# Spacing a single-channel gather a quarter of a step apart, and moving one batch's load and folds earlier, in an FFT and MLP kernel

## Chip, cores, metric

Each kernel runs on one core of a Trainium2 chip. The metric is device time in microseconds (us). Each timed run is one execution; a kernel's figure is the median of its runs. All timed runs quoted here were classed as fast. The experiments were timed in four groups, on three different chips, so every ratio is taken against runs of the kernel before in the same group. Two experiments (after_look and folds_look) are single runs for a trace, and a single run has no known state; they are marked where they are used, and no verdict rests on them alone.

## The reference, cut to what matters

```python
# x: (8, 3008, 256); w_in: (256, 2048); w_out: (2048, 256); all float32
X = np.fft.fft(np.fft.fft(x, axis=1), axis=2).real      # FNet mixing
h = X.reshape(24064, 256) @ w_in
g = np.where(h > 0, h, np.exp(np.minimum(h, 0)) - 1)    # ELU
out = g @ w_out
```

## The kernel before

The program is a pipeline of 376 steps (47 tiles of 512 tokens, eight steps each) of about 4.75 us; in the source a step is T = 4.8. The Fourier transform of the next batch and all side work are put between by a list of events, `at(time, function)`. `time` is only a place in program order. An instruction wrapped in `pin` keeps its place on its queue; an unpinned transfer may be moved along its queue by the scheduler. So the program order in the source is not the order of SyncE's queue.

The real transform uses symmetry, so channel 128 needs its own column of x: one element out of each row of 256, 8 batches by 3008 rows. Those elements are copied singly, 192 rows at a time ("a piece"), 4 pieces to a quarter. A finished quarter goes to a DRAM scratch tensor (`xe_dr`) and returns in another layout (`xs`):

```python
def load_ext(j, s0, s1):                       # quarter j, rows s0 to s1
    if j == 0 and s0 == 0:
        state["x1"] = spool.tile([128, HALF + 1], FP, tag="rx", bufs=1, name="x1")
    t = state["x1"][j * NB : (j + 1) * NB]     # 8 partitions, one per batch
    def copy(s0, s1, row, step):
        pin(nc.sync.dma_start(
            out=t[:, s0:s1],
            in_=bass.AP(tensor=xt, offset=x.offset + row * ND + 128,
                        ap=[[SEQ * ND, NB], [step * ND, s1 - s0], [1, 1]])))
    ...                                        # one quarter has a piece of a single row more
    if s1 == 768:
        nc.sync.dma_start(out=xe_dr[j], in_=t[:, 0:768])        # not pinned

def get_ext():
    xs = state["xs"] = spool.tile([128, 4, NB, 6], FP, tag="xs", bufs=1, name="xs")
    for j in range(4):                                          # not pinned
        nc.sync.dma_start(out=xs[:, j], in_=xe_dr[j].rearrange("b (p m) -> p b m", m=6))

def fold_ext():                                # GpSimd: three additions make xe
    ...
def dft_ext():                                 # TensorE: 24 matmuls with xe as weights
    ...
```

Four other parts share the queues. Two are DMA traffic: the stores of finished output tiles, 40 transfers for the first two tiles (24 of them 32 KB each, all on SyncE), and a later batch's x, in four transfers:

```python
def load_x(b):
    for j in (2, 1):                           # indirect loads, issued by GpSimd
        load = nc.gpsimd.indirect_dma_start(out=L[j], ...)
        if b == 1:
            pin(load)
    nc.sync.dma_start(out=L[3], in_=xrows(b, HALF, 6, 128))     # SyncE, 768 KB each
    nc.sync.dma_start(out=L[0], in_=xrows(b, 0, 6, 128))
```

Two are GpSimd work: folds (additions of x with its mirror image) and sums of weights. The events concerned:

```python
for i in range(8):
    at((13 + 0.6 * i) * T + 3.6, lambda i=i: sum_weights(i))
...
for n in range(16):
    j, k = divmod(n, 4)
    at((14.4 + 0.62 * n) * T, lambda j=j, k=k: load_ext(j, 192 * k, 192 * (k + 1)))
at(25.0 * T, get_ext)
at(26 * T + 1.35, fold_ext)
at(26 * T + 4.75, dft_ext)
...
for b in range(1, NB):
    s0 = (b - 1) * steps_b
    l0 = s0 - 8 if b > 1 else 5.2
    at(l0 * T + 0.1, lambda b=b: state.update(L=load_x(b)))
    f0, f1 = (s0 - 1, s0 + 38) if b > 1 else (8, 37)
    ...                                        # folds spread evenly over steps f0 to f1
```

## Time and profile before

| | before |
|---|---|
| median of 3 runs (range) | 1985.48 us (1985.08 to 1985.95) |
| TensorE busy, in the profiled run | 1958.8 of 1985.3 us |
| TensorE's wait for xe | 11.89 us, until 192.88 us |

The profiled run itself took 1987.05 us, 1.6 us more than the median; this will matter. The prediction below shows the lines of the slices, waits, stretches and SyncE's queue on which this table rests, and works out from them what the stall costs and how long the quarters of the gather took. One line is wanted beside them. It is from GpSimd's timeline of the kernel before (start, us, engine, line, operation, out<-in, count, and in brackets what ended the idle time ahead of it):

```profile
173.68 1.00 POOL L157 DMA_INDIRECT xl<-in_x_dram,ix  x1 [0.27 <-POOL o L476]
```

This is the first of GpSimd's own two loads of batch 2's x. It is issued 3.9 us after the last quarter's first piece, and on another queue than the gather's, so it cannot be seen in SyncE's queue. How the two kinds of view are read together decides this case: a queue's timeline tells when transfers are issued, and only the next entry that waits for them tells when they landed (the last four pieces left the queue by 181.46 us, 169.82 + 11.64; the xe_dr that waits for them was issued at 187.58).

### The profile page before, as it was taken

What the parts mean: (1) busy time and instruction counts of PE and PEld (TensorE: products, weight loads), DVE (VectorE), ACT (ScalarE), POOL (GpSimd) and SP (SyncE); (2) the same over time, 40 slices, a digit from 0 to 9 for tenths busy, and PEclk for the clock granted to TensorE, in tenths of its full rate; (3) what the DMA queues carried; (4) which work ended last, traced back from release to release, by engine and by line L of the source; (5) the groups of instructions that cost most, each with busy time, mean ns of one, the idle gap of its engine ahead of it and who ended that gap; (6) DMA issues with size and microseconds to landing.
All of it is one profiled execution on the core that took longest, in us unless ns stands there. A gap on an engine that the chain in (4) does not pass through costs nothing.

```text
span 1985.3 us, 26858 instructions
## 1 busy us (share of the span) xinstructions
PE 1958.8 (99%) x8912; PEld 1656.7 (83%) x8912; DVE 1278.8 (64%) x2325; ACT 869.4 (44%) x1668; POOL 1362.2 (69%) x1800
## 2 busy tenths in 40 slices
PE   9997999999999999999999999999999999999998
PEld 5786888888888888888888888888888888888887
DVE  8864666675666656666566665666566665566666
ACT  4643434444444444444444444444444444344443
POOL 3696757786587765877667875678757776455665
PEclk9998999999999999999999999999999999999999
DMA  8135111121001110011100211013010010100101
GB/s 331 54 34 60 44 16 17 39 59 21 13 15 51 43 30 13 18 43 46 28 11 19 59 30 27 11 19 85 10 21 11 19 22 14 16 12 12 22 10 24
DMA packets 255546, 71.01 MB, mean 36 GB/s; under 512 B 243934, under 2 KB 244850, under 8 KB 255024
## 3 DMA queue, kind: packets, MB, share of 16 engines
q1 hardware_dynamic: 250896, 56.46, 14.3%
q0 software_dynamic: 2336, 12.59, 2.0%
q8 instruction: 70, 1.15, 0.2%
q14 instruction: 68, 0.56, 0.1%
q10 hardware_dynamic: 2176, 0.26, 0.1%
HBM read 44.43 MB, written 24.80 MB: 35 GB/s over the span
## 4 chain that ended last, share of the span: by engine, by line
PE 94%; DVE 2%; DMA 2%; SPq 1%; POOL 1%; issue 1%; ACT 0%; POOLq 0%; DVEq 0%; ACTq 0%
PE H L382 38%; PE pD L382 16%; PE pB L382 16%; PE pC L382 16%; PE pA L382 8%; DMA x<-in_x_dram 1%; PE M L382 1%; SPq L988 1%; POOL G L391 1%; DVE E L764 0%; SPq L613 0%; DVE G L790 0%; DVE v L388 0%; DVE pow L281 0%; DVE Ir L388 0%
## 5 line engine op out<-in xcount | busy, mean ns | idle before, releaser
L391 POOL TENSOR_TENSOR G<-G 128x256 f32<-128x256 f32 x1440 | 1037.1, 730 | 545.0 <-DVE G L790 436.3
L764 DVE SCALAR_TENSOR_TENSOR E<-Rb,wex,H 128x256 f32<-128x256 f32 x752 | 327.8, 477 | 618.2 <-PE H L382 614.4
L394 ACT ACTIVATE G<-H 128x512 f32<-128x512 f32 x376 | 224.6, 597 | 951.1 <-DVE G L774 951.1
L382 PE MATMUL H<-Ir,Ws 128*128 128x256 f32 x1504 | 387.3, 380 | 1.3 <-DVE E L764 1.3
L382 PE MATMUL H<-Rr,Wc 128*128 128x256 f32 x1504 | 387.6, 380 | 0.0
L382 PE MATMUL pC<-G,WT 128*128 128x256 f32 x1440 | 369.5, 379 | 0.0
L382 PEld LDWEIGHTS H<-Rr,Wc 128*128 128x128 f32 x1504 | 285.0, 190 | 56.9 <-issue 4.0
L382 PEld LDWEIGHTS H<-Ir,Ws 128*128 128x128 f32 x1504 | 277.8, 189 | 50.3 <-DVE E L764 4.7
L382 PEld LDWEIGHTS pC<-G,WT 128*128 128x128 f32 x1440 | 273.6, 190 | 37.2
L774 DVE SCALAR_TENSOR_TENSOR G<-E,H 128x512 f32<-128x512 f32 x376 | 256.9, 683 | 39.5 <-PE H L382 2.9
L790 DVE SCALAR_TENSOR_TENSOR G<-G,H 128x512 f32<-128x512 f32 x376 | 255.5, 680 | 28.7 <-ACT G L394 28.6
L790 DVE SCALAR_TENSOR_TENSOR G<-M,G 128x512 f32<-128x512 f32 x376 | 256.6, 683 | 0.0
L394 ACT ACTIVATE G<-G 128x512 f32<-128x512 f32 x376 | 233.2, 620 | 0.0
L382 PE MATMUL pA<-G,w 128*128 128x256 f32 x784 | 229.4, 379 | 0.7 <-DVE G L790 0.7
L382 PE MATMUL pB<-G,w 128*128 128x256 f32 x784 | 229.3, 379 | 0.0
L382 PE MATMUL pD<-G,w 128*128 128x256 f32 x784 | 229.3, 379 | 0.0
L394 ACT ACTIVATE M<-G 128x512 f32<-128x512 f32 x376 | 223.9, 595 | 0.0
L394 ACT ACTIVATE M<-M 128x512 f32<-128x512 f32 x376 | 220.9, 588 | 0.0
L382 PE MATMUL pB<-G,WT 128*128 128x256 f32 x720 | 214.8, 380 | 3.2 <-POOL G L391 3.2
L382 PE MATMUL pD<-G,WT 128*128 128x256 f32 x720 | 214.4, 379 | 1.5 <-DVE v L388 1.5
L382 PEld LDWEIGHTS pA<-G,w 128*128 128x128 f32 x784 | 148.9, 190 | 21.3 <-DVE G L790 1.1
L382 PEld LDWEIGHTS pB<-G,w 128*128 128x128 f32 x784 | 149.0, 190 | 20.3
(140 smaller groups left out, 1407.9 us busy)
## 6 DMA issues: line engine op xcount, KB each, us to landing
out_dram<-ot SPq DMA_DIRECT2D x496, 32.0 KB
xl<-in_x_dram SPq DMA_DIRECT2D x16, 768.0 KB
out_dram<-ot SPq DMA_DIRECT2D x256, 2.0 KB
Rb<-r SPq DMA_DIRECT2D x10, 376.0 KB
raw<-in_moe_w_in_dram SPq DMA_DIRECT2D x7, 512.0 KB
MC<-dft_mats SPq DMA_DIRECT2D x3, 1131.0 KB
raw<-in_moe_w_out_dram SPq DMA_DIRECT2D x4, 512.0 KB
out_dram<-ot SPq DMA_DIRECT2D x64, 28.0 KB
```

What stands on the lines that cost most here:

```text
L382: nc.tensor.matmul(out_, lhsT=lhsT, rhs=rhs, start=start, stop=stop, skip_group_check=True)
L391: pin(nc.gpsimd.tensor_tensor(out=o, in0=a, in1=b, op=op))
L394: pin(nc.scalar.activation(out=o, in_=i, func=func, **kw))
L764: nc.vector.scalar_tensor_tensor(out=S.E[:, c], in0=Rb[:, cols(i)], scalar=wex[:, f : f + 1], in1=S.H[:, c], op0=ALU.mult, op1=ALU.add,)
L774: nc.vector.scalar_tensor_tensor(out=two(S.G[:, 0:512])[:, :, ::-1], in0=two(S.E), scalar=2.0, in1=two(S.H), op0=ALU.mult, op1=ALU.subtract,)
L790: nc.vector.scalar_tensor_tensor(out=o, in0=e, scalar=-1.0, in1=h, op0=ALU.add, op1=ALU.max)
L988: queue.dma_start(out=bass.AP(tensor=out.tensor, offset=out.offset + r0 * ND + half * 128 + 32 * g, ap=[[2 * ND, w], [64 * ND, nb], [1, 32 ...
```

## The change

The intent: close the gather up, so that it ends before TensorE wants it, and move GpSimd's work on batch 1 out of the time when TensorE waits for GpSimd. No arithmetic and no byte is added or removed.

```diff
     for i in range(8):
-        at((13 + 0.6 * i) * T + 3.6, lambda i=i: sum_weights(i))
+        at((12.9 + 0.5 * i) * T + 3.6, lambda i=i: sum_weights(i))
 ...
         at(
-            (14.4 + 0.62 * n) * T,
+            (14.4 + 0.25 * n) * T,
             lambda j=j, k=k: load_ext(j, 192 * k, 192 * (k + 1)),
         )
 ...
-        l0 = s0 - 8 if b > 1 else 5.2
+        l0 = s0 - 8 if b > 1 else 3.2
         at(l0 * T + 0.1, lambda b=b: state.update(L=load_x(b)))
-        f0, f1 = (s0 - 1, s0 + 38) if b > 1 else (8, 37)
-        at(f0 * T, lambda b=b: begin_folds(b))
+        first = (6, 7, 7, 8, 9, 9, 10, 10, 12, 15)
+
+        def fold_slot(n):
+            if b > 1:
+                return s0 - 1 + 39 * n // n_big
+            return first[n] if n < len(first) else 17 + int(0.92 * (n - len(first)))
+
+        at(fold_slot(0) * T, lambda b=b: begin_folds(b))
 ...
-            slot = int(f0 + n * (f1 - f0) / n_big)
+            slot = fold_slot(n)
```

## The prediction

> **What bounds the kernel now.** I read the page first. TensorE is busy 1958.8 of 1985.3 us, and the chain that ended last is 94% TensorE. So the floor of this program is about 1959 us, and a change that adds and removes no TensorE work can at best win back part of the 26.5 us in which TensorE is idle. The slices say where to look:
>
> ```profile
> PE   9997999999999999999999999999999999999998
> ...
> PEclk9998999999999999999999999999999999999999
> ```
>
> Each slice is 49.6 us. The fourth (149 to 198 us) is the only one below 9 in the TensorE row, apart from the last, and the only one whose granted clock is below 9. Next, the waits of 130 to 200 us, as engine, line, what it waited for, us in total, times, longest:
>
> ```profile
> POOL xs L391 <- DMA xs<-xe_dr: 13.2, 1, 13.2
> PEld H L382 <- POOL xe L391: 12.3, 1, 12.3
> PE H L382 <- POOL xe L391: 11.9, 1, 11.9
> ...
> PE pB L382 <- POOL G L391: 2.2, 2, 1.6
> ```
>
> TensorE stands still once for 11.9 us, because GpSimd has not made xe, because GpSimd waits 13.2 us for xs. That is the gather of channel 128: load_ext copies single elements of x into one tile, each quarter goes through DRAM (xe_dr) and returns as xs, fold_ext adds, dft_ext multiplies. The busy table by stretches (first columns: window, us, TensorE busy with its count; further on the granted clock) prices the stall:
>
> ```profile
> 181.00:184.60 3.60, 0.00 (x0) 0.00 (x0) 0.00 (x0) 0.85 (x2) 0.00 (x0) 1.00 0.80 3
> 184.60:192.80 8.20, 0.00 (x0) 0.00 (x0) 0.00 (x0) 0.00 (x0) 0.65 (x3) 0.50 0.43 105
> 192.80:198.30 5.50, 5.42 (x27) 2.50 (x28) 0.00 (x0) 1.17 (x3) 5.20 (x9) 0.50 0.00 0
> 198.30:205.00 6.70, 6.70 (x32) 5.86 (x32) 4.95 (x10) 1.98 (x4) 4.78 (x6) 1.00 0.41 122
> ```
>
> After 3.6 us of idleness the clock is halved, and the first 5.4 us of work run at half speed: another 2.7 us lost. The stall costs 11.9 + 2.7 = **14.6 us** in all. Last, the queue of SyncE that issues the gather (start, us in the queue, what, count):
>
> ```profile
> 113.58 6.30 SPq L613 DMA_DIRECT2D x<-in_x_dram  x4
> 126.05 0.28 SPq L631 DMA_DIRECT2D xe_dr<-x  x1
> 126.37 0.64 SPq L613 DMA_DIRECT2D x<-in_x_dram  x2
> 127.74 0.79 SPq L637 DMA_DIRECT2D xs<-xe_dr  x1
> 132.75 5.40 SPq L988 DMA_DIRECT2D out_dram<-ot  x12
> 138.19 0.35 SPq L613 DMA_DIRECT2D x<-in_x_dram  x1
> ...
> 166.10 2.10 SPq L168 DMA_DIRECT2D xl<-in_x_dram  x1
> 169.46 0.30 SPq L631 DMA_DIRECT2D xe_dr<-x  x1
> 169.82 11.64 SPq L613 DMA_DIRECT2D x<-in_x_dram  x4
> ...
> 189.76 0.37 SPq L637 DMA_DIRECT2D xs<-xe_dr  x1
> ```
>
> The reader should see that quarter one is done by 126 us, then the pieces stand between stores of the first two output tiles, and the last four pieces are issued only after 169.8 us, behind batch 2's x (L168). They land at 187.58 us, 17.8 us after their first issue, against 12.5 us for the first quarter alone (113.58 to 126.05).
>
> [...] 243934 of 255546 packets are under 512 B, and a piece of 8x192 elements (6 KB) takes some 3.1 us in a full quarter (12.5 / 4). [...]
>
> **The change, part by part.** The built programs give the new order on each queue; durations are those of the rows above.
>
> Gather. Still 17 issues, no bytes saved. In the new SyncE order quarters one to three stand before all stores; then come 12 stores, 2 pieces, 12 stores, 2 pieces, 3 stores, the fourth xe_dr, 13 stores, the fourth xs, and only then batch 2's x. The queue waits at each xe_dr for its quarter to land. Starting at 113.6 (the issue ahead of it, the last wex, is unmoved):
> - three quarters at 12.5 us, plus some 1.4 us of earlier xs traffic in between: third xe_dr at about 152.5; its xs must wait for that to land (2.16 us in the row of the chain), so 155;
> - 12 stores 5.4 us, two pieces 0.7, 12 stores 6.2 plus about 1.5 of back-pressure behind the pieces (before, 3 and 5 stores behind one piece took 2.38 and 3.71 us instead of 1.5 and 2.5): 169; two pieces and 3 stores: 172;
> - the two pieces land about 6.5 us after issue (2 x 3.1): fourth xe_dr at 176;
> - 13 stores at 0.49 us: 182.5 to 183; the fourth xs, then 3.12 us to TensorE's first matmul (192.88 - 189.76 before): **about 185.8**, against 192.88. Gain 7.1 us. Without the 13 stores between xe_dr and xs it would be near 179.
>
> Batch 1's x and its folds. GpSimd has the same instructions. The indirect loads go from 63.6 to about 51 us, into an almost idle DMA stretch. Eight half folds (1.2 to 1.36 us each), not five, stand ahead of about 105 us; fewer stand among the weight sums. GpSimd is 97% busy from 120 to 140 us (19.37 of 20.00) and TensorE waits for its G there, 1.63 us at 138.86 and 0.59 at 144.46. With some 3 us of folds gone from in front and the sums spaced 0.5 steps instead of 0.6, both should vanish: 2.2 us. But this only brings TensorE to dft_ext at 178.8 instead of 181.0; it still waits for xe until 185.8. So **it adds nothing to the total as long as the gather is late**.
>
> Clock. The remaining stall is 185.8 - 178.8 = 7 us, long enough for the halving again. I count +0.5 us as a mean of "as before" and "not halved".
>
> Sum: 1985.5 - 7.1 - 0.5 = 1977.9; I put 1977.5. After dft_ext nothing moves in the order of TensorE, and 1.33 us of small stalls at 215 to 217 us should stay.
>
> **Rivals.**
> - *The gather ends before TensorE arrives.* For it: pieces stand much closer, and batch 2's x leaves the way. Against: 13 stores ahead of the last xs. It would win all: 11.9 + 2.7 + 2.2 = 16.8 us, 1968.7.
> - *The stores held back by the gather pay it back.* They start at 155 instead of 132.75 us. Against: the output tile has two buffers and the third transpose comes after dft_ext, near 190 us, when all are issued. If it failed, VectorE would wait and TensorE lose some us: 1982 or so.
> - *VectorE becomes the bound at 80 to 105 us.* It is 91% busy (18.18 of 20.00), TensorE waits 0.2 us for its E at 105.53, and more GpSimd folds lie beside its two-input operations. This could cost 1 to 2 us and would shift the gather's start as well: 1979.
> - *Nothing gained*: small pieces in a row choke the queue, and xe comes at 192 as before: 1985.
>
> **Range and chances.** Resumption between 180 and 190 us, and the clock's luck of up to 2.7 us, give 1970 to 1983 for 8 in 10. Two per cent would be 39.7 us. The whole idle time is 26.5 us, so faster by over 2% is impossible in practice; slower by 2% would need a stall three times the present one.
>
> **What would show it.** TensorE's wait for xe: 11.9 falls to about 7 (right), to 0 (first rival), or stays. The last xs issued near 183 us. The GpSimd waits at 138.86 and 144.46 gone. The clock low again beside dft_ext. I am wrong if the early part (before 113 us) gets longer, if xe arrives before 179 us, or if steady state after 230 us changes at all.

## The result, and the profile after

The changed kernel took 1985.47 us (median of 4 runs, 1980.86 to 1986.63), the kernel before 1985.28 (4 runs, 1984.86 to 1985.95). The ratio is 0.9996, with a 95% interval of 0.9979 to 1.0014. Ratios here are the mean time of one kernel's fast runs over that of the other's of the same rounds, so not quite the ratio of the medians. The result is "within 2%", as predicted, but no gain could be measured, and 1985.47 lies above the predicted range of 1970 to 1983.

The profiled run happened to be the fastest of the four, 1980.86 us. In its slices the TensorE row and the clock row now read:

```profile
PE   9998999999999999999999999999999999999998
...
PEclk9998999999999999999999999999999999999999
```

The fourth slice has risen from 7 to 8 and is still the weak one. The waits of 100 to 205 us after the change (engine, line, what it waited for, us in total, times, longest):

```profile
POOL xs L391 <- DMA xs<-xe_dr: 9.3, 1, 9.3
PEld H L382 <- POOL xe L391: 8.4, 1, 8.4
PE H L382 <- POOL xe L391: 8.0, 1, 8.0
...
PE pB L382 <- POOL G L391: 1.1, 1, 1.1
```

It is the same chain: TensorE waits for GpSimd's xe, GpSimd for xs, and xs for the gather. Only 3.9 us of it is gone. The stretches around it (window, us, TensorE busy, and further on the granted clock):

```profile
179.00:182.20 3.20, 0.13 (x1) 0.00 (x0) 0.00 (x0) 1.00 (x2) 0.00 (x0) 1.00 0.46 72
182.20:187.00 4.80, 0.00 (x0) 0.00 (x0) 0.00 (x0) 0.00 (x0) 0.60 (x2) 0.50 0.64 110
187.00:192.40 5.40, 5.28 (x27) 2.38 (x28) 0.00 (x0) 1.02 (x3) 4.97 (x8) 0.50 0.56 230
```

After 3.1 us of idleness (3.6 before) the clock was halved, and the first 5.3 us of work ran at half speed (5.4 before). SyncE's queue of the kernel after:

```profile
111.87 6.45 SPq L613 DMA_DIRECT2D x<-in_x_dram  x4
124.39 0.28 SPq L631 DMA_DIRECT2D xe_dr<-x  x1
124.72 7.31 SPq L613 DMA_DIRECT2D x<-in_x_dram  x5
...
139.78 0.28 SPq L631 DMA_DIRECT2D xe_dr<-x  x1
...
152.72 0.28 SPq L631 DMA_DIRECT2D xe_dr<-x  x1
...
169.69 1.82 SPq L613 DMA_DIRECT2D x<-in_x_dram  x2
171.62 2.61 SPq L988 DMA_DIRECT2D out_dram<-ot  x3
177.09 0.28 SPq L631 DMA_DIRECT2D xe_dr<-x  x1
177.42 6.52 SPq L988 DMA_DIRECT2D out_dram<-ot  x13
183.98 0.45 SPq L637 DMA_DIRECT2D xs<-xe_dr  x1
```

One line each of GpSimd's and of TensorE's timeline belong to it:

```profile
171.84 1.00 POOL L157 DMA_INDIRECT xl<-in_x_dram,ix  x1 [0.27 <-POOL o L476]
187.12 4.18 PE L382 MATMUL H<-MC,xe 128*8 128x377 f32 x24 [7.99 <-POOL xe L391]
```

The order is what the built program showed: three quarters, then stores with two pairs of pieces between them, the fourth xe_dr, thirteen stores, the last xs. In this run the moments are near the predicted ones (third xe_dr 152.72 against 152.5, fourth 177.09 against 176, last xs 183.98 against 182.5 to 183). GpSimd's load of batch 2's x is issued at 171.84 us, 2.2 us after the first of the last two pieces. So this run confirms the picture, and the other three runs were slower than it by some 4.5 us or more. The question for the experiments is what those runs did.

### The profile page after: what moved, and what is told of

It is laid out like the page before. It is cut to its first block, busy times and chain, and to the rows that moved or that the text cites. A ratio compares the mean times of both kernels' runs of the same rounds, so it can differ in the third digit from the quotient of the medians.

```text
span 1979.1 us, 26862 instructions
## 1 busy us (share of the span) xinstructions
PE 1957.6 (99%) x8912; PEld 1656.3 (84%) x8912; DVE 1277.2 (65%) x2325; ACT 869.5 (44%) x1668; POOL 1363.8 (69%) x1800
## 3 DMA queue, kind: packets, MB, share of 16 engines
q1 hardware_dynamic: 250896, 56.46, 14.6%
## 4 chain that ended last, share of the span: by engine, by line
PE 94%; DVE 2%; POOL 1%; DMA 1%; issue 1%; SPq 0%; ACT 0%; DVEq 0%; POOLq 0%
PE H L382 38%; PE pB L382 16%; PE pC L382 16%; PE pD L382 16%; PE pA L382 8%; POOL WT L391 1%; DMA out_dram<-ot 0%; SPq L988 0%; DMA xl<-in_x_dram,ix 0%; DVE e L476 0%; POOL w L391 0%; DVE E L764 0%; POOL G L391 0%; DVE v L388 0%; DVE pow L281 0%
## 5 line engine op out<-in xcount | busy, mean ns | idle before, releaser
L382 PEld LDWEIGHTS pD<-G,w 128*128 128x128 f32 x784 | 149.0, 190 | 20.3
```

What stands on the lines that cost most here:

```text
L382: nc.tensor.matmul(out_, lhsT=lhsT, rhs=rhs, start=start, stop=stop, skip_group_check=True)
```

## The experiments

A yardstick first. In ten traces in which TensorE waits for xe and the last xs has a line of its own, the time is the moment of the last xs plus 1795.7 to 1797.3 us: before 1987.05 - 189.76 = 1797.3, after 1980.86 - 183.98 = 1796.9, and so on down to the worst, after_look, 1995.50 - 198.47 = 1797.0. So a run's time tells when its last xs was issued. By this estimate the median run of after (1985) had it near 188 us, and so had the median run of before.

The runs of before beside the experiments had medians of 1985.15 (51 runs), 1985.42 (34), 1985.72 (11) and 1984.38 us (9), one for each group of kernels timed together, on chips 12, 4, 2 and 12 of the record. Apart from dram_early, every kernel timed was within 2% of before; what tells them apart are the intervals of the ratios. All results were correct.

### 1. after_again: the change again, more runs

No edit.

> The changed kernel once more, unchanged, because its four runs on record fall apart (1980.9 once, 1985.4 to 1986.6 three times) where the kernel before stays within 1.1 us. Theory A (the wait for xe shrinks from 11.9 to about 8 us in every run, and the rest is luck of the clock): all runs between 1979 and 1983. Theory B (two modes: in most runs something else is lost that the recorded trace of the 1980.9 us run does not show): runs again in two clumps, some near 1981 and some near 1985.5; if the profiled run is a slow one, its trace shows the lost 5 us, either as a wait for xe of 11 us or more, or as a later start of the gather.

Measured: 1984.99 us (13 runs, 1978.3 to 1987.52), ratio 0.9996 (0.9988 to 1.0004). The traced run took 1983.27 us. Lines of SyncE's queue from its trace:

```profile
170.72 1.76 SPq L613 DMA_DIRECT2D x<-in_x_dram  x2
172.58 2.93 SPq L988 DMA_DIRECT2D out_dram<-ot  x3
180.50 0.28 SPq L631 DMA_DIRECT2D xe_dr<-x  x1
```

The third xe_dr is as early as in the first trace (152.29 us), but the last two pieces took 9.8 us to land (170.72 to 180.50) in place of 7.4. There is no mean gain to explain away: over 17 timed runs the change spreads from 1978 to 1988 us, and only two of them are below 1983.

### 2. gather_only and 3. folds_only: the two halves of the change

gather_only is the kernel before with `0.62` changed to `0.25`; folds_only is the changed kernel with `0.25` put back to `0.62`.

> The kernel before with the closer gather alone (pieces a quarter of a step apart); loads, folds and weight sums as before. SyncE has the same order of gather, stores and batch 2's x as the changed kernel. Theory A: the gather alone carries the gain; last xs issued at about 185, wait for xe shrinks to about 6 us because TensorE arrives 1 to 2 us later than in the changed kernel, time as the changed kernel, 1979 to 1983. Theory B (folds matter for the gain): 1985, as before.

> The changed kernel with the old spacing of the gather (0.62 of a step); batch 1's x early, folds and weight sums as changed. Theory A: no gain, since TensorE only arrives 2 us earlier at the same late xe: wait for xe about 14 us, time 1985 to 1986. Theory B (the folds carry the gain): wait for xe 12 us or less, time 1981 to 1983.

Measured: gather_only 1985.64 us (22 runs, 1979.36 to 1986.67), ratio 0.9991 (0.9985 to 0.9998); its runs lie in two clumps, 8 at 1979.4 to 1982.7 and 14 at 1984.9 to 1986.7. In its trace (1985.74 us) TensorE waits 12.7 us for xe, where about 6 had been expected. folds_only 1987.97 us (21 runs), ratio 1.0013 (1.0006 to 1.0019). TensorE's timeline of folds_only, the gaps at the first and at the long wait (the traced run took 1991.56 us, 3.6 more than the median):

```profile
137.78 0.70 PE L382 MATMUL pB<-G,WT 128*128 128x256 f32 x2 [1.07 <-POOL G L391]
...
198.06 4.18 PE L382 MATMUL H<-MC,xe 128*8 128x377 f32 x24 [19.00 <-POOL xe L391]
```

The fold half does to GpSimd what it was meant to: the first wait is 1.07 us (1.63 before) and the second, 0.59 us at 144.46, is gone. TensorE arrives at dft_ext at 198.06 - 19.00 = 179.1 us, not 181.0, and merely waits longer. So that half adds nothing while the gather is late. That it loses 2.8 us was not expected. In its trace the third xe_dr is issued at 173.31 us (169.46 before), and in a further look, **folds_look** (one run, state unknown, 1991.65 us), at 172.10 us. There, five stores behind a piece took 5.87 us, 3.71 before.

> One more trace of the changed kernel with the old spacing of the gather, which was 2.8 us slower than the kernel before in its median. Its first trace lost 4 us in the third quarter (fourth of the stretch 154 to 173 us) against the kernel before. If that is its rule, the third xe_dr is again issued at 172 us or later; if it was chance, at 168 to 170 and the wait for xe falls to 15 us.

Why those transfers are slower when folds and sums lie elsewhere was not settled.

One side effect does show. In after, after_again, after_look and folds_only the gather's first issue comes 6.80 us after the matmul that follows the small TensorE gap at 105 us; in before, gather_only and before_x2_held (below) 8.05 or 8.06 us after it. So the fold half starts the gather 1.25 us sooner, where the prediction had called that start unmoved.

### 4. after_look: the change, one more trace

No edit; one run, state unknown.

> One more trace of the changed kernel, for the durations of its quarters and last two pieces beside its time. Theory A (the time follows the moment of the last xs): the span is 1979.1 + 0.5 to 1 times what the fourth xe_dr is later than 177.1 us. Theory B: no relation.

It took 1995.5 us, slower than any timed run of this kernel, so it shows where the time can go, not how often. The first two quarters in SyncE's queue:

```profile
111.99 8.06 SPq L613 DMA_DIRECT2D x<-in_x_dram  x4
128.63 0.28 SPq L631 DMA_DIRECT2D xe_dr<-x  x1
128.96 8.44 SPq L613 DMA_DIRECT2D x<-in_x_dram  x5
...
146.37 0.28 SPq L631 DMA_DIRECT2D xe_dr<-x  x1
```

A quarter that took 12.5 us in other traces takes 16.6 and 17.4 here, with the same issues in the same order. The table gathers every trace with the spacing of 0.25. A quarter runs from its first piece's issue to its xe_dr's issue; "pair" is the last two pieces, counted in the same way.

| trace | first quarter | second | third | third xe_dr to pair | pair | last xs at |
|---|---|---|---|---|---|---|
| after | 12.5 | 15.1 | 12.6 | 17.0 | 7.4 | 184.0 |
| after_again | 12.5 | 14.5 | 12.4 | 18.4 | 9.8 | 187.1 |
| gather_only | 12.5 | 17.6 | 12.3 | 18.0 | 9.3 | 190.1 |
| after_look | 16.6 | 17.4 | 16.1 | 20.2 | 8.9 | 198.5 |
| hold_x2 (below) | 14.3 | 17.4 | 12.4 | 17.5 | 6.7 | 189.0 |
| predicted | 12.5 | 12.5 | 12.5 | 16.5 | 6.5 to 7 | 182.5 to 183 |

The kept traces also hold a record of every DMA packet, and this narrows the cause. While the first quarter of after_look ran (111.99 to 128.63 us), the core's DMA engines moved 6448 packets, 0.03 MB, all from the gather: no other transfer of this kernel lay beside it, and still it took 16.6 us. The first quarters of before and of after moved 6448 packets too, every one of 4 bytes, in 12.5 us. The packets themselves are what differs. A full quarter holds 42 to 48 packets that took over 1 us each, with a mean of 1.20 to 1.25 us in the quarters of 12.3 to 12.6 us and of 1.64 to 1.70 us in those of 16.1 to 17.5 us.

### 5. single_moved: is it the tiny piece?

The second quarter has five pieces, one of them a single row. This kernel issues that one ahead of the first quarter, into the same place; the other pieces stay.

```diff
             if j == 1 and s0 == 0:
-                copy(0, 1, 0, 1)
                 copy(1, s1, SEQ - 1, -1)
```

> The changed kernel, with the one-element piece of the second quarter (row 0 of each batch) moved ahead of the first quarter. The second quarter took 14.5, 15.1 and 17.5 us in three traces, the first and the third 12.3 to 12.6 in all. Theory A (the fifth, tiny piece costs the 2 to 5 us): the second quarter takes 12.5 us, the first 14.5 or more. Theory B (place or direction of the second quarter): the first stays at 12.5 and the second at 14.5 or more. Time within 2 us of the changed kernel, since this moves xe by at most the difference.

Measured: 1983.4 us (20 runs, 1976.97 to 1989.16), ratio 0.9985 (0.9976 to 0.9994). The second quarter still took 15.8 us in the trace (125.37 to 141.13), the first 12.3. So the fifth piece is not what makes a quarter slow.

### 6. hold_x2: GpSimd's load of batch 2's x out of the way

The rival reading of the late pair is contention, which means that two transfers hold each other up: the load at 171.84 us. Pinned, GpSimd's two loads of batch 2 stay at step 39, long after dft_ext.

```diff
-            if b == 1:
+            if b in (1, 2):
                 pin(load)
```

> The changed kernel, with GpSimd's two loads of batch 2's x kept at step 39, where the program asks for them; in the changed kernel the first of them is issued at 171.8 us, beside the last two pieces of the gather. All other orders are the same. Theory A (the last two pieces, 7.4 and 9.8 us to land in two traces instead of the 6.5 that I had put, are slowed by this load): they land within 6.5 us, xe comes 1 to 3 us earlier, median 1981 to 1983 and a narrower spread. Theory B (the gather of single elements is slow and uneven by itself): no change, median 1985.

Measured: 1980.61 us (12 runs, 1975.87 to 1985.93), ratio 0.9971 (0.9962 to 0.9979); before beside it 1985.42. The traced run was its slowest, with the slow early quarters of the table. Yet its pair was the fastest of all (SyncE's queue):

```profile
175.70 1.81 SPq L613 DMA_DIRECT2D x<-in_x_dram  x2
177.60 2.41 SPq L988 DMA_DIRECT2D out_dram<-ot  x3
182.40 0.28 SPq L631 DMA_DIRECT2D xe_dr<-x  x1
```

6.7 us is nearly the predicted 6.5. In the five traces of the changed spacing with the load beside it (after, after_again, gather_only, single_moved and, below, xs_ahead) the pair took 7.4 to 9.8 us. So part of the missing gain is this load: the kernel is faster without it. It is issued by GpSimd (at 171.84 us in after) and the pieces by SyncE, and still the pair took 7.4 us beside it in after and 6.7 us without it here. How much of the gain runs through the pair is less sure. 6.7 us is one trace; in after_look the load was issued 11 us ahead of the pair, and the pair took 8.9 us without it, in a run whose quarters were all slow; and the median lies 4.8 us under that of before, more than the 0.7 to 3.1 us by which the pairs differ.

### 7. before_x2_held: the same cure for the kernel before

The kernel before, with all four loads of batch 2's x pinned at step 39, and nothing else of the change.

```diff
-            if b == 1:
+            if b in (1, 2):
                 pin(load)
-        nc.sync.dma_start(out=L[3], in_=xrows(b, HALF, 6, 128))
-        nc.sync.dma_start(out=L[0], in_=xrows(b, 0, 6, 128))
+        late = pin if b == 2 else (lambda load: load)
+        late(nc.sync.dma_start(out=L[3], in_=xrows(b, HALF, 6, 128)))
+        late(nc.sync.dma_start(out=L[0], in_=xrows(b, 0, 6, 128)))
```

> The kernel before, with all four loads of batch 2's x kept at step 39; in the kernel before, one of SyncE's and one of GpSimd's stand beside the last quarter of the gather, which took 17.8 us against 12.5 for the first. Theory A (these loads slow the last quarter): last quarter 12.5 to 13.5 us, xe 4 to 6 us earlier, median 1979 to 1981. Theory B (the last quarter is slow by itself): 1985.

Measured: 1979.97 us (7 runs, 1979.37 to 1980.52), ratio 0.997 (0.9959 to 0.9981). SyncE's queue at the last quarter:

```profile
168.81 6.20 SPq L614 DMA_DIRECT2D x<-in_x_dram  x4
175.05 3.33 SPq L638 DMA_DIRECT2D xs<-xe_dr  x1
182.21 0.28 SPq L632 DMA_DIRECT2D xe_dr<-x  x1
183.84 0.38 SPq L638 DMA_DIRECT2D xs<-xe_dr  x1
```

The last quarter takes 13.4 us, 17.8 before, and the median falls by 5.7 us with the old spacing. What made the last quarter late in the kernel before was thus mostly batch 2's x. And the runs spread by only 1.2 us, although the first quarter was slow in the trace (13.7 us). Where the pieces stand apart between stores, that quarter did not delay the next in this trace: the second xe_dr was issued at 154.57 us, 155.15 in before. Whether that is why the runs spread so little was not shown.

### 8. xs_ahead: the thirteen stores

The changed kernel with everything on SyncE's queue in this stretch pinned, so that the last xs follows the last xe_dr at once; batch 2's SyncE loads wait too. GpSimd's do not.

```diff
+            pin(nc.sync.dma_start(out=xe_dr[j], in_=t[:, 0:768]))     # and each xs
...
+                    if q < 2:
+                        pin(copied)                                    # stores of tiles 0 and 1
...
-    at(25.0 * T, get_ext)
+    at(18.155 * T, get_ext)
```

> The changed kernel, with the last xs before the 13 stores (stores of the first two tiles, xe_dr, xs and SyncE's x of batch 2 kept in program order). Theory A (the place of the 13 stores in SyncE's queue costs 13 x 0.49 = 6.4 us of the wait): the last xs is issued 2 us after the fourth xe_dr, wait for xe about 3 to 6 us instead of 8 to 12, median 1977 to 1980. Theory B (the stores cost nothing there, the transfer itself sets the wait): median 1985.

Measured: 1976.11 us (6 runs, 1971.15 to 1982.45), ratio 0.9951 (0.9934 to 0.9967). In its trace the second quarter took 17.0 us although no xs lay beside it, and the pair 8.5 (SyncE's queue):

```profile
170.25 1.76 SPq L614 DMA_DIRECT2D x<-in_x_dram  x2
178.77 0.28 SPq L632 DMA_DIRECT2D xe_dr<-x  x1
179.09 2.37 SPq L639 DMA_DIRECT2D xs<-xe_dr  x4
```

And from TensorE's timeline:

```profile
184.40 4.18 PE L383 MATMUL H<-MC,xe 128*8 128x377 f32 x24 [5.25 <-POOL xe L392]
```

From the issue of the fourth xe_dr to TensorE's first matmul with xe it is 5.6 us here, against 10.0 in after and 9.7 in after_again. So the thirteen stores do stand on the path, and cost it some 4 us; the other 2 us or so of their 6.6 in the queue the last xs would have waited anyway, until xe_dr had landed (2.16 us in before's trace). The median fell by 9 us; where the rest of that came from no trace shows. And with quarters of 12 or 17 us ahead of them, even this kernel spreads over 11 us.

### 9. gather_first, and again as first_again: the whole gather ahead of all stores

The pieces at 0.16 steps, xs at step 17, pinned as in xs_ahead.

```diff
-            (14.4 + 0.25 * n) * T,
+            (14.4 + 0.16 * n) * T,
...
-    at(25.0 * T, get_ext)
+    at(17.0 * T, get_ext)
```

> The changed kernel, with all 16 pieces, xe_dr and xs in SyncE's queue before any store (pieces 0.16 of a step apart, stores of the first two tiles in program order). The gather starts at 112 us and needs four quarters of 12.5 to 17.5 us: the last xs lands at about 170, before TensorE comes at 179. Theory A: no wait for xe, clock 1.00 throughout, median 1969 to 1971, spread under 2 us, and the stores that move to 168 us cost nothing. Theory B (stores held back pay it back): VectorE's transpose of the third tile waits for its buffer near 190 us, or the stall moves elsewhere: median above 1975.

> The gather-first kernel again, for its spread and another trace. Theory A (gather durations of 12.3 to 17.4 us a quarter, now hidden up to about 179 us): most runs 1969 to 1971.5, a few up to 1977 when the four quarters together exceed some 64 us. If the trace is of such a run, it shows a wait for xe of under 7 us and quarters over 15 us. Theory B: the outliers have no wait for xe, but another one.

Measured: 1970.93 us (5 runs, 1969.95 to 1976.19), ratio 0.9938 (0.9925 to 0.9951), and again 1970.78 (5 runs, 1970.32 to 1975.91), ratio 0.9931. In the first trace TensorE doesn't wait for xe at all and its clock is full there: the 24 matmuls with xe take 2.09 us, 4.18 in after, and the mean granted clock is 0.999. The second trace is of the run of 1975.91 us and shows both a late gather and a rival of the prediction at work. From SyncE's timeline of that run, the first stores:

```profile
174.96 22.25 SPq L990 DMA_DIRECT2D out_dram<-ot  x40
```

From VectorE's timeline, the transpose into an output tile:

```profile
191.49 0.71 DVE L937 STREAM_TRANSPOSE ot<-u 128x512 f32<-128x512 f32 x1 [5.18 <-DMA out_dram<-ot]
```

And from TensorE's, what waited for VectorE in turn:

```profile
193.01 2.08 PE L382 MATMUL H<-Ir,Ws 128*128 128x256 f32 x4 [3.60 <-DVE E L766]
```

Two of its four quarters were slow (17.0 and 16.3 us), so the stores began at 174.96 us; 165.61 in the first trace. VectorE's transpose waited 5.18 us for the stores to free its buffer, and TensorE 3.60 us for VectorE, after which the clock was halved once more: these four matmuls took 2.08 us, 1.03 before the wait (for xe itself TensorE waited only 0.70 us). "The stores held back by the gather pay it back" did happen in this trace, where the stores began 9.35 us later than in the first, which has no such wait. With the change as made, no such wait shows either.

### 10. dram_early: no SBUF on the way

Pieces copied straight from x to the DRAM scratch, from step 8. It would take away the landing in between and the tile that the gather has to wait for. In after's trace the DMA engines lie idle from 68 to 98 us, with a busy share of 0.00 to 0.02 in 10 us stretches.

```diff
-                    out=t[:, s0:s1],
+                    out=xe_dr[j][:, s0:s1],
...
-            (14.4 + 0.25 * n) * T,
+            (8.0 + 0.25 * n) * T,
...
-    at(25.0 * T, get_ext)
+    at(16.0 * T, get_ext)
```

> The changed kernel with the gather copied straight from DRAM to DRAM (no tile on the chip in between, so it need not wait for the tile that the weights and batch 0's row use), issued from step 8 on, in a stretch in which the DMA engines idle; xs comes back before the stores. If the late xe is the whole stall, the wait for xe is 0, the clock stays at 1.00 there, and the time is 1985.5 - 11.9 - 2.7 - up to 2 = 1969 to 1971. If something else stands right behind xe (stores, GpSimd), the stall moves and the time stays above 1975.

Measured: 2117.88 us (5 runs), ratio 1.0668: a miss by far. Eight pieces in SyncE's queue:

```profile
133.41 61.29 SPq L609 DMA_DIRECT2D xe_dr<-in_x_dram  x8
```

And the longest of four gaps of 12 to 69 us in TensorE's timeline:

```profile
219.83 2.07 PE L382 MATMUL H<-Ir,Ws 128*128 128x256 f32 x4 [69.15 <-DVE E L758]
```

A piece took 61.29 / 8 = 7.7 us here from DRAM to DRAM (5.0 ns an element), not some 3.1. The small loads that VectorE needs (wex) stood behind the pieces in the same queue, and TensorE waited up to 69 us for VectorE.

### 11. early and 12. early_four: a tile of its own, and pieces earlier

The gather's tile shares its buffer with another (tag "rx"), so it cannot start earlier. Both kernels give it a small tile of its own with 8 partitions for each piece, pinned as in gather_first. early puts eight pieces between the loads of wex, from 86 us on; early_four only four at 85.5 us, and the others after the last wex. The pieces then go to xe_dr in 16 transfers, after the last of them.

```diff
-            state["x1"] = spool.tile([128, HALF + 1], FP, tag="rx", bufs=1, name="x1")
+            state["x1"] = spool.tile([128, 192], FP, tag="x1", bufs=1, name="x1")
...
-            (14.4 + 0.25 * n) * T,
+            ((10.1 + 0.15 * n) if n < 4 else 13.1 + 0.14 * (n - 4)) * T,     # early_four
```

> As the run with the gather ahead of the stores, and in addition the gather has a small tile of its own (128x192, 768 bytes a partition) and its first eight pieces go out from about 98 us on. The last xs then lands some 20 us before TensorE asks for xe. Theory A (the two of five runs at 1974.9 and 1976.2 us of the gather-first kernel came from a gather so slow that xe was late again): all runs within 1969 to 1971.5. Theory B (those 5 us come from something else): again single runs near 1975.

> As the early gather, but only the first four pieces go out early (from 86 us, right after a wex; the 1977.9 us run kept them from disturbing the wex of 98 us), and the other twelve follow the last wex, so no wex stands behind pieces. Theory A (the 6.4 us wait for E at 123.6 us came from the last wex standing behind five pieces in the DMA rings, and the outliers of the gather-first kernel from a slow gather): no wait at 123 us, none for xe, clock 1.00, all runs 1969 to 1971.5. Theory B: an outlier near 1975 again, or a wait of over 2 us somewhere.

Measured: early 1977.93 us (5 runs, 1977.18 to 1978.7), ratio 0.9961 (0.9947 to 0.9975). TensorE doesn't wait for xe, but its timeline has something new:

```profile
123.63 2.07 PE L382 MATMUL H<-Ir,Ws 128*128 128x256 f32 x4 [6.42 <-DVE E L775]
```

wx, issued at 114.68 us behind five pieces, landed so late that wex, which reads it, was issued only at 120.55; in other traces wex follows wx after 1.1 to 1.2 us. That is the lesson of dram_early in small, and early_four avoids it: 1969.7 us (5 runs, 1969.67 to 1970.49), ratio 0.9928 (0.9914 to 0.9941). SyncE's queue:

```profile
111.85 28.96 SPq L614 DMA_DIRECT2D x<-in_x_dram  x13
140.86 8.07 SPq L636 DMA_DIRECT2D xe_dr<-x  x16
148.98 2.25 SPq L647 DMA_DIRECT2D xs<-xe_dr  x4
151.28 19.72 SPq L999 DMA_DIRECT2D out_dram<-ot  x40
```

All xs are issued by 151.2 us, 28 us before TensorE wants xe. The stores end at 171 us. No long wait is left (the longest of TensorE between 100 and 205 us is 1.0 us), the clock stays at full (mean granted clock 1.0, the 24 matmuls with xe in 2.09 us), and the runs agree within 0.8 us. It beats before by some 14 to 15 us, and was the best kernel found.

## Why the prediction was right or wrong

**The bound and the price of the stall: right.** 14.6 us were to be had from stall and clock, and 1968.7 us if all was won. early_four, with no stall, takes 1969.7 us.

**The new order of the queue, and what sets the end: right.** Time follows the last xs to within 2 us in ten traces. The thirteen stores ahead of it take 6.6 to 6.9 us in the queue, predicted 6.5 to 7; from the last xs to TensorE it is again 3.1 us.

**Folds and batch 1's x: right in the main.** The waits of 1.63 and 0.59 us fell to 1.08 and 0, so half of the predicted 2.2 us was won; TensorE arrives at 179.1 us, predicted 178.8, and waits. folds_only shows that this half gains nothing alone. The rival of VectorE as the bound did not come true: TensorE's gap near 105 us is 0.48 us, 0.20 before. GpSimd work does go with slower VectorE operations in before's trace: between 60 and 110 us three of the L281 operations (two inputs, 128x512) began ahead of a GpSimd addition and took 0.68 us, and five began during one, took 0.84 to 2.38 us and ended 0.54 to 0.56 us after it. That this could cost 1 to 2 us was the author's estimate.

**The step that failed** is the gather's sum: "three quarters at 12.5 us", and then "the two pieces land about 6.5 us after issue". Both terms were taken from the first quarter of one trace, which ran with little beside it. The runs showed in their place:

- a quarter takes 12.3 to 17.6 us from run to run, so 2.0 to 2.9 ns an element (6144 of them). The second took 14.4 us or more in all five traces of the table. Three quarters took 40 to 51 us from first issue to third xe_dr, against 38.9 predicted;
- the stretch from the third xe_dr to the pair (its xs, 24 stores, two pieces) took 17.0 to 20.2 us, against 16.5;
- the pair takes 7.4 to 9.8 us. "Batch 2's x leaves the way" held for SyncE's two loads and not for GpSimd's, which is issued beside the pair in two of the three traces of the changed kernel; GpSimd's timeline of before (the line at 173.68 us) would have told. Without that load the pair took 6.7 us in the one trace, and the median falls to 1980.61. But a slow pair can also come without it (after_look, 8.9).

Counted from the first piece, the last xs comes 3 to 17 us later than predicted in the three traces of the changed kernel; the first piece itself was issued 1.3 to 1.7 us earlier than predicted. In after_again, of the three the one nearest the median, the quarters add 1.1 us, the stretch of stores 1.9 and the pair some 3. A median run has its last xs near 188 us, not 183.

**Smaller slips.** The prediction took a gain read off a trace of a 1987.05 us run from a median of 1985.48; by the yardstick a last xs at 182.75 would have meant about 1979.6, not 1977.5, even had all durations been right. And the half microsecond for luck with the clock: after the wait TensorE again ran 5.3 us at half speed. The clock was low for 13.65 us in before's trace and 10.24 in after's. Further traces have 6.83 (before_x2_held), 20.48 (folds_only) and 23.89 us (after_look). These are 4, 3, 2, 6 and 7 times 3.41 us. Why they come in such steps was not shown; the half microsecond was the author's estimate. "Without the 13 stores between xe_dr and xs it would be near 179" left out that xs has to wait for xe_dr to land, 2.16 us by the prediction's own row: xs_ahead shows some 4 us for the stores, not 6.8. And a slowdown by 39.7 us would need a stall of 3.7 times the present 14.6 us, not of three times.

**Why the median did not move.** In the kernel before, the late end came mostly from the last quarter beside batch 2's x, as before_x2_held shows. The change takes SyncE's half of that traffic away, but puts three quarters back to back, where a slow one delays all that follows (third xe_dr at 162.79 us in after_look, 152.72 in after), and thirteen stores between the last xe_dr and the last xs. One wait was exchanged for another of about the same length, with more spread. The rival "nothing gained" had the right outcome (1985) but only part of the cause: pieces in a row do run slower at times, but not always.

**Open.** Why the same quarter takes 12.3 us or 17.6 was not found. It isn't the single-row piece (single_moved), not traffic of xs beside it (xs_ahead), and it can happen with no other transfer of this kernel beside it (the first quarter of after_look, a single run); nor does the second place in the row always make a quarter slow (12.6 us in gather_first). folds_only's late third quarter shows the same sign as the slow ones, 32 packets of over 1 us with a mean of 1.64 us against 1.23 in before, so it may be the same thing; that isn't shown. Nor is it known why gather_only falls into two clumps.

## What to carry to other kernels

When a wait hangs on many tiny transfers, take their durations from several places and several runs, and look on every engine's queue for what is issued beside them; one clean block of one trace gave the lower edge here and not the mean (12.5 us, where the traces have 12.3 to 17.6). Before closing a gather up, look for the large load that lies beside its last part: moving that load alone gained 5.7 us here, where closing up gained nothing. To win the rest, get the last dependent transfer ahead of bulk stores and leave it tens of us of slack (28 us in early_four, whose runs agree within 0.8 us), but keep small, urgent loads of the same queue ahead of the slow pieces (behind them TensorE waited 6.42 us in early and 69.15 in dram_early).
